# One FFN matmul fewer between a digit's counts and their sum in the second routing round

## The chip, the cores and the metric

The kernel runs on one core of a Trainium2 chip. The metric is the device time of one execution in microseconds (us); the median of several executions is quoted. Engines: TensorE (PE, its weight loads PEld), VectorE (DVE), ScalarE (ACT), GpSimd (POOL), SyncE (SP). A list of executions also gives each one's span (the time, less some 1.8 us) and its mean granted TensorE clock, where 1 is full speed.

## The reference, cut to what matters

```python
y = gated_linear_attention(q, k, v, f_logit)       # 4 batches, 8 heads, 768 steps, 48 wide
x = y.transpose(0, 2, 1, 3).reshape(3072, 384)     # one row per token
logits = x @ w_gate                                # 3072 x 8 experts
for idx in np.argsort(-logits.flatten()):          # greedy, best pair first
    tok, e = idx // 8, idx % 8
    if assigned[tok] < 0 and counts[e] < 384:      # each expert takes 384 tokens
        assigned[tok] = e; counts[e] += 1
for e in range(8):
    h = np.maximum(x[assigned == e] @ w1[e], 0)    # 384 -> 1024
    out[assigned == e] = h @ w2[e]                 # 1024 -> 384
```

## The kernel before: the parts that matter

After the attention part the routing runs in eight rounds, numbered 0 to 7. A round searches a threshold digit by digit (five digits), makes the list of one expert's tokens, gathers their rows and puts that expert's FFN, in 51 pieces, into a queue. A piece is a transposition of 128 gathered rows (three transposes), or one FFN matmul in fp32 (two records in the trace). TensorE takes pieces from the queue at fixed places of the next round, beside the small matmuls of the search.

```python
def digit_beside(above, choice, size, slots):
    some(pe_work, slots[0])              # FFN pieces before the counts
    ...                                  # three matmuls "cnt" (L758): the counts
    ...                                  # VectorE: own, part, parts
    some(pe_work, slots[1])              # FFN pieces between counts and their sum
    nc.tensor.matmul(out=cnt, lhsT=ones[0:m, :], rhs=parts...)      # the sum (L773)
    ...                                  # VectorE: fills, filled, sized, the next digit's "above"

def assign(choice, over, pick, slots):
    ...
    some(pe_work, slots[0])
    nc.tensor.matmul(out=r[:, 0:E], lhsT=ones[:], rhs=count[:], ...)   # "sums" (L819)
    some(pe_work, slots[1])

def tokens():                            # the list is made; its rows are gathered
    ...
    pieces, last = ffn(L), []
    if len(pe_work) >= 12:               # hold two old matmuls back, between the transposes
        last = [pe_work.pop() for _ in range(2)][::-1]
    pe_work.extend(pieces[:TE - 1] + last[:1] + pieces[TE - 1:TE] + last[1:] + pieces[TE:])

pace = {0: None, 1: (2, 2)}
for rnd in range(E - 1):
    slots, more = pace.get(rnd, (3, 2)), 3 if rnd > 1 else 0
    ...                                  # five digits, the first with `more` pieces more
    assign(choice, over, pick, (3, 7))
    ...                                  # nine steps of the list, with 1 or 2 pieces after each
```

## Time and profile before

| | before |
|---|---|
| time, three runs | 478.16 us (477.72 to 478.54) |
| span of the profiled run | 474.0 us, mean clock 0.967 |
| TensorE busy | 93% of the span |
| VectorE, ScalarE, GpSimd busy | 55%, 29%, 28% |
| list to list, rounds 2 to 6 | 36.9 to 37.0 us, once 38.62 |

The rows of waits name who waited for whom, and the order of work gives each instruction's start and length, with the idle time before it in brackets. Two consecutive records of an FFN matmul start 0.32 us apart though each is shown 0.5 us long, because a record runs to a modelled end; so the idle times are somewhat short. The lines themselves stand in the prediction.

### The profile page before, as it was taken

To read this page: it belongs to the slowest core of one execution; us is meant where nothing else is said; L and a number is where in the kernel's file an instruction comes from. 1 tells how busy PE (TensorE), PEld (TensorE's weight loads), DVE (VectorE), ACT (ScalarE), POOL (GpSimd) and SP (SyncE) were. 2 spreads that over 40 slices of the span, in tenths; PEclk is the share of its full clock that TensorE was granted. 3 is DMA by queue.
4 is the path that set the end of the run, shared out by engine and by line. 5 is a ranking of instruction groups with operands and counts; after the bars stand their busy time and mean duration, and the time that the engine had idled before them with its cause. 6 is when DMAs were issued, how large, how long until landed. Compare 5 with 4: busy or idle time off the path is not lost. (4 is left out here: it accounts for less than half of the span.)

```text
span 474.0 us, 11870 instructions
## 1 busy us (share of the span) xinstructions
PE 439.3 (93%) x4854; PEld 296.1 (62%) x4854; DVE 262.2 (55%) x890; ACT 139.0 (29%) x322; POOL 131.3 (28%) x190
## 2 busy tenths in 40 slices
PE   8999999999998489998998998998998998999994
PEld 4788889899887344554564564554554555555552
DVE  5788767788796757555555636726735656000000
ACT  4666646566641011102202202212202211212200
POOL 1556546565530030051042023023014015201001
PEclk9999989999999569999999999999998999999998
DMA  8999988888111071271071082072072046800001
GB/s 171 204 202 201 198 188 179 176 176 191 55 46 54 3 253 64 67 256 44 13 293 62 0 297 70 0 283 83 2 271 94 1 168 193 324 0 35 17 17 39
DMA packets 118399, 59.11 MB, mean 125 GB/s; under 512 B 101664, under 2 KB 112960, under 8 KB 118336
## 3 DMA queue, kind: packets, MB, share of 16 engines
q1 hardware_dynamic: 111760, 44.06, 35.4%
q0 software_dynamic: 3072, 9.44, 6.1%
q10 hardware_dynamic: 3504, 4.77, 2.8%
q8 instruction: 40, 0.66, 0.6%
q14 instruction: 23, 0.19, 0.1%
HBM read 48.77 MB, written 9.49 MB: 123 GB/s over the span
## 5 line engine op out<-in xcount | busy, mean ns | idle before, releaser
L1021 PE MATMUL H<-xeT,w 128*128 128x384 f32 x384 | 136.7, 503 | 4.0 <-ACT xeT L1013 4.0
L1021 PEld LDWEIGHTS H<-xeT,w 128*128 128x128 f32 x384 | 68.6, 192 | 45.8 <-issue 6.2
L1038 POOL DMA_INDIRECT out_dram<-o,token x21 | 22.6, 1074 | 204.8 <-ACT o L1037 200.6
L1033 PE MATMUL O<-w,hT 128*128 128x384 f32 x192 | 64.8, 489 | 0.0
L1033 PE MATMUL last_O<-w,hT 128*128 128x384 f32 x192 | 64.7, 489 | 0.0
L1025 ACT ACTIVATE hT<-H 128x384 f32<-128x384 f32 x64 | 31.4, 490 | 113.0 <-PE H L1021 113.0
L1033 PEld LDWEIGHTS last_O<-w,hT 128*128 128x128 f32 x192 | 35.9, 190 | 25.0 <-issue 1.4
L1033 PEld LDWEIGHTS O<-w,hT 128*128 128x128 f32 x192 | 35.8, 190 | 24.0 <-issue 0.7
L313 DVE COPY_PREDICATED am<-mask,A 128x512 f32<-128x512 int32 x48 | 32.4, 731 | 14.6 <-PE A L308 14.6
L237 POOL TENSOR_TENSOR kg<-k,ek 128x384 f32<-128x384 f32 x23 | 23.1, 1004 | 49.3 <-ACT ek L215 49.3
L308 PE MATMUL A<-qT,kT 48*64 48x128 f32 x768 | 26.8, 273 | 1.1 <-ACT gl L247 0.7
L323 PE MATMUL Y<-v,am 128*64 128x48 f32 x768 | 27.0, 223 | 0.3 <-DVE am L313 0.3
L323 PEld LDWEIGHTS Y<-v,am 128*64 128x64 f32 x768 | 24.6, 138 | 1.4 <-DVE am L313 0.8
L978 POOL DMA_INDIRECT xe<-xd,token x21 | 22.3, 1060 | 8.4 <-issue 4.3
L191 POOL TENSOR_TENSOR low<-g,upper 128x384 fp32r<-128x384 f32 x22 | 22.2, 1008 | 7.3 <-DVE upper L188 5.6
L308 PEld LDWEIGHTS A<-qT,kT 48*64 48x64 f32 x768 | 21.4, 133 | 1.8 <-issue 0.9
L1013 ACT COPY xeT<-Xe 128x384 f32<-128x384 f32 x24 | 11.3, 480 | 36.9 <-PE Xe L1010 36.8
L127 PE MATMUL nothing<-idle,ones 128*128 128x384 bf16 x77 | 20.4, 408 | 1.7 <-DVE ones L132 1.5
L1037 ACT COPY o<-O 128x384 f32<-128x384 f32 x12 | 5.7, 478 | 54.2 <-PE O L1033 54.2
L1037 ACT COPY o<-last_O 128x384 f32<-128x384 f32 x11 | 5.3, 478 | 54.6 <-PE last_O L1033 48.6
L214 ACT ACTIVATE eq<-dl 128x384 f32<-128x384 f32 x24 | 12.6, 524 | 27.4 <-DVE dl L212 27.4
L1010 PE MATMUL Xe<-ident,xe 128*128 128x128 f32 x72 | 12.4, 286 | 6.8 <-DMA xe<-xd,token 6.8
(218 smaller groups left out, 648.2 us busy)
## 6 DMA issues: line engine op xcount, KB each, us to landing
w<-in_moe_w_dram SPq DMA_DIRECT2D x16, 1536.0 KB, 6.7
f<-in_f_logit_dram SPq DMA_DIRECT2D x24, 192.0 KB, 4.3
q<-in_q_dram SPq DMA_DIRECT2D x24, 192.0 KB, 3.8
k<-in_k_dram SPq DMA_DIRECT2D x24, 192.0 KB, 4.4
v<-in_v_dram SPq DMA_DIRECT2D x24, 192.0 KB, 3.6
xd<-x ACTq DMA_DIRECT2D x24, 192.0 KB, 2.9
xe<-xd,token POOLq DMA_INDIRECT x21
out_dram<-o,token POOLq DMA_INDIRECT x21
```

The costliest lines, as they stand in the source:

```text
L127: nc.tensor.matmul(out=nothing[:, 0:CAP], lhsT=ones[:], rhs=idle[:], start=True, stop=True)
L191: nc.gpsimd.tensor_tensor(out=low[:], in0=g[:, :, 0:DH], in1=upper[:].bitcast(FP32), op=ALU.subtract)
L214: nc.scalar.activation(out=G["eq"][:], in_=dl[:], func=AF.Exp, bias=0.0, scale=-1.0)
L237: engine.tensor_tensor(out=G["kg"][:, :, 0:DH], in0=G["k"][:], in1=G["ek"][:], op=ALU.mult)
L308: nc.tensor.matmul(out=A[par][HC * j:HC * j + HC, 128 * hp:128 * hp + 128], lhsT=G["kT"][rows, hp, HC * j:HC * j + HC], rhs=G["qT"][rows, ...
L313: nc.vector.copy_predicated(am[:, par], mask[:].unsqueeze(1).to_broadcast((128, HP, 128)), A[par][:].rearrange("s (a t) -> s a t", t=128))
L323: nc.tensor.matmul(out=Y[par][HC * j:HC * j + HC, DH * hp:DH * hp + DH], lhsT=G["am"][:, par, hp, HC * j:HC * j + HC], rhs=G["v"][:, 2 * h ...
L978: nc.gpsimd.indirect_dma_start(out=xe[:], out_offset=None, in_=xd[:, :], in_offset=bass.IndirectOffsetOnAxis(ap=token[:, i:i + 1], axis=0))
L1021: nc.tensor.matmul(out=L["H"][:, 0:CAP], lhsT=L["w1"][:, d, 128 * ft:128 * ft + 128], rhs=xT[:, d, :], start=(d == 0), stop=(d == DC - 1))
L1025: nc.scalar.activation(out=hT[:, ft, :], in_=L["H"][:, 0:CAP], func=AF.Relu)
L1033: nc.tensor.matmul(out=L["O"][:, 0:D], lhsT=hT[:, ft, 128 * i:128 * i + 128], rhs=L["w2"][:, ft, :], start=(ft == 0), stop=(ft == FC - 1))
L1038: nc.gpsimd.indirect_dma_start(out=outs[next(tiles)][:, :], out_offset=bass.IndirectOffsetOnAxis(ap=L["token"][:, i:i + 1], axis=0), in_=o ...
```

## The change

Round 1 has fewer FFN pieces to spare than later rounds, since nothing was left from round 0. The intent is to use one less in each of its digits, so that more are left when its list is made and TensorE has work until the rows arrive.

```diff
-            pace = {0: None, 1: (2, 2)}
+            pace = {0: None, 1: (2, 1)}
```

## The prediction

> **What bounds the kernel now.** I read the page first, then TensorE's waits from 176 us on, TensorE's order of work in the second and third round, and the granted clock around one stall. The page says who is busy:
>
> ```profile
> PE 439.3 (93%) x4854; PEld 296.1 (62%) x4854; DVE 262.2 (55%) x890; ACT 139.0 (29%) x322; POOL 131.3 (28%) x190
> ```
>
> TensorE sets the end, so only its idle time can be won. The kernel has an attention part (up to some 154 us), which the change does not touch, and a routing part of eight rounds, numbered here 0 to 7. A round finds one expert's tokens on VectorE and GpSimd while TensorE works off the FFN of the expert before, taken piece by piece from a queue. What TensorE waits for in the routing part (columns: who waited for whom, us in total, times, longest):
>
> ```profile
> PE Xe L1010 <- DMA xe<-xd,token: 6.8, 11, 0.9
> PE H L1021 <- ACT xeT L1013: 4.0, 7, 0.6
> PE cnt L758 <- DVE above L527: 1.1, 4, 0.3
> PE sums L819 <- DVE count L530: 1.1, 6, 0.2
> PE before L892 <- DVE member L524: 0.3, 1, 0.3
> ```
>
> The first two are one bubble: TensorE reaches the transposes of the gathered rows (L1010) before the gather has landed, and the first FFN matmul (L1021) then waits for ScalarE's copy of the transposes. In time order, at the start of round 2 (start us, us, engine, line, what; in brackets the idle time before):
>
> ```profile
> 207.48 0.75 PE L963 MATMUL tokens<-number,in_line 128*128 128x6 bf16 x24
> 208.08 5.41 PE L1033 MATMUL O<-w,hT 128*128 128x384 f32 x16
> 213.33 0.25 PE L758 MATMUL cnt<-choice,above 128*128 128x64 bf16 x3
> 213.41 0.53 PE L1010 MATMUL Xe<-ident,xe 128*128 128x128 f32 x3
> 214.37 0.55 PE L1010 MATMUL Xe<-ident,xe 128*128 128x128 f32 x3 [0.43 <-DMA xe<-xd,token]
> 214.76 0.22 PE L773 MATMUL cnt<-parts,ones 128*128 128x128 bf16 x1
> 215.74 0.55 PE L1010 MATMUL Xe<-ident,xe 128*128 128x128 f32 x3 [0.76 <-DMA xe<-xd,token]
> 216.85 1.56 PE L1021 MATMUL H<-xeT,w 128*128 128x384 f32 x4 [0.57 <-ACT xeT L1013]
> 218.25 0.25 PE L758 MATMUL cnt<-choice,above 128*128 128x64 bf16 x3
> ...
> 221.75 0.25 PE L758 MATMUL cnt<-choice,above 128*128 128x64 bf16 x3
> ```
>
> The list of tokens is made at 207.48. Only 8 FFN matmuls (16 records, two to a matmul) lie between it and the transposes. The gather's issues on GpSimd:
>
> ```profile
> 211.22 0.97 POOL L978 DMA_INDIRECT xe<-xd,token  x1 [0.30 <-issue]
> 212.49 1.10 POOL L978 DMA_INDIRECT xe<-xd,token  x1 [0.30 <-issue]
> ```
>
> The second ends at 212.19 and its transposes start at 214.37; the third 213.59, then 215.74. So rows are there 2.2 us after the issue ends. Rounds 2 to 7 show the same three gaps (0.3 to 0.5, 0.6 to 0.9 and 0.57 us).
>
> Now round 1, where the change is; one digit:
>
> ```profile
> 185.12 0.26 PE L758 MATMUL cnt<-choice,above 128*128 128x64 bf16 x3 [0.29 <-DVE above L527]
> ...
> 185.98 0.29 DVE L520 TENSOR_TENSOR parts<-part,pick_th 128x128 bf16<-128x128 bf16 x1
> ...
> 186.59 0.22 PE L773 MATMUL cnt<-parts,ones 128*128 128x128 bf16 x1
> ...
> 188.44 0.26 PE L758 MATMUL cnt<-choice,above 128*128 128x64 bf16 x3 [0.29 <-DVE above L527]
> ```
>
> From counts to sum (185.12 to 186.59) TensorE is the later one: the parts are done at 186.27, but two FFN matmuls stand ahead of the sum. From sum to the next counts (1.86 us) VectorE is.
>
> **What the Trainium skill says.** "DMA: Bandwidth & Descriptors", section on the anatomy of a GpSimd DMA, gives a fixed cost of about 2 us; "Perfetto Trace Analysis", summary of the profiler window, says such a record ends when the descriptors are generated, not when data has moved. Both agree with the 2.15 to 2.2 us above. "TensorE: Matmul & The Clock Gate", "What's actually happening", says that TensorE's clock falls to half after an idle window, and that windows of 3413 ns run freely. The trace has this once in the routing part, right after round 6's bubble, for some 3.4 us (window; time, busy PE, PEld, DVE, ACT, POOL; then the clock):
>
> ```profile
> 364.50:365.00 0.50, 0.21 (x1) 0.22 (x2) 0.09 (x1) 0.23 (x1) 0.00 (x0) 0.63 0.00 0
> 367.50:368.00 0.50, 0.50 (x5) 0.49 (x4) 0.09 (x1) 0.00 (x0) 0.00 (x0) 0.50 0.00 0
> ```
>
> Lists are at 207.48, 244.47, 281.44, 318.37, 355.36 and 393.98: rounds of 36.9 to 37.0 us, and one of 38.62. The dip costs 1.65 us.
>
> **The change part by part.** It takes one FFN matmul from each of round 1's five digits. Replaying the queue by hand: round 0 adds 51 pieces (3 transposes, 24 up, 24 down) and uses 2. Round 1 takes 5x4 for digits, 10 around its sums and 11 up to the list: 8 are left. With (2, 1) it is 5x3, and 13 are left. Rounds 2 to 6 each take as many as they add, 51, so every later list finds 13 too instead of 8. And the code that holds the last two matmuls back, to put them between the transposes, needs at least 12; it never applied up to round 6 and now applies everywhere.
>
> Sizes: an FFN matmul is 0.645 us (8 of them, 451.66 to 456.82, take 5.16); plus 0.09 after counts (218.33 to 219.71 is two, 1.38) and 0.055 after a sum (219.76 to 221.75 is three, 1.99); a transpose piece is 0.33 (two, 433.72 to 434.37).
>
> *Round 1.* The sum starts when the parts are done (counts + 1.15 + 0.06 for the signal = 1.21) instead of at 1.47: 0.26 saved in four digits. In the first, parts end at 179.56, so 179.62 for 179.94: 0.32. The list is 1.36 us earlier. VectorE's 1.86 us stays.
>
> *Rounds 2 to 6*, from the list at 0. Before: counts 5.85, next counts 10.77, third counts 14.27 (221.75 - 207.48). After: tokens and 8 down matmuls again, counts at 5.85; two down matmuls, sum at 7.31; one down matmul and two transposes end at 7.37 + 0.70 + 0.65 = 8.72, but VectorE lets the counts start only at 7.31 + 1.86 = 9.17 (a new wait, 0.45); one down matmul and the third transposes end at 10.31, sum at 10.38; the last down matmul and two up end at 10.44 + 0.70 + 1.29 = 12.43, the third counts. The copy of the transposes is ready at 9.98 + 1.11 = 11.09 (from 215.74 to 216.85), before the up matmuls at 11.14. The same work is done at the third counts in both, so each round saves 14.27 - 12.43 = 1.84; five save 9.20.
>
> The gather is not late: the store that stood before it on GpSimd (208.43) now comes after, so issues start about 1.4 after the list, and rows land at about 4.7, 6.0 and 7.3 for use at 8.07, 8.4 and 9.98.
>
> *Round 7.* VectorE still sets the matmul "before" at 5.68 (399.66 - 393.98); 4 down matmuls and 2 transposes end at 9.03, the second list waits for VectorE's last in_line (403.00, so 9.08), then down, transposes, down, and up matmuls from 11.54, where the copy is ready. Before, they went on at 11.27 (405.25) with two of them done. So the end lies 11.54 + 1.29 - 11.27 = 1.56 later after round 6's list; that is the five deferred matmuls (3.2) less the bubble.
>
> Sum: -1.36 - 9.20 + 1.56 = -9.0 us. In TensorE's idle time: about 2 us more in round 1, 11 us less later.
>
> *Clock.* Without the bubble I expect no dip. The bubbles come 37 us, or 10.8 windows, apart, so they walk through the window's phases in six rounds and about one should be hit in most runs. I count 0.8 x 1.65 = 1.3 us, and take off 0.4 for what I have not seen: 478.16 - 9.0 - 1.3 + 0.4 = 468.3.
>
> **Rivals.** (1) Only time moved: five matmuls are deferred, TensorE is 93% busy, and round 1 loses as much as is won, about 478. Against it: 10.8 us of waits stand in the first two rows of the waits, and all but round 1's go. (2) The new wait is larger: with fewer matmuls beside it, VectorE's digit chain becomes the bound, in round 1 and in the second digit of each later round. That is in my sum (0.39 and 0.45 us a time); were it double in the later rounds, 2.6 us would go, leaving some 471. (3) The gather lands later since it now runs beside other transfers; it has over 2 us of slack, so it would take twice the issue-to-landing time to cost anything. (4) The clock: dips in more rounds of the timed runs than of the profiled one (475.83 against 478.16 us) would make the gain larger, 466 or 467; low activity in round 1 could bring a new dip, but TensorE still works about 72% of each digit there.
>
> **Range and chances.** The sum without the clock is 469.2, with one dip removed 467.5; 2% is 468.6, just between. The sum's own errors are some 0.2 us in each of five rounds. Range 466.2 to 471.0. Over 2% faster 0.54, within 2% 0.45, slower 0.01.
>
> **What would show it.** In the changed profile: the wait of L1010 for the gather gone from the waits, that of L1021 for the copy near zero except round 1's; a new wait of the sum (L773) for parts, about 0.2 to 0.4 us, in round 1; counts to counts there 3.06 instead of 3.32 us; lists from round 1 to 6 35.1 us apart; third counts 12.4 us after each list; a wait of under 0.5 us before each round's second counts; no clock of 0.5 after 180 us. Wrong it would be if the lists stay 37 us apart (the gather is late all the same) or TensorE's waits for VectorE grow past 5 us in total.

## The result, and the profile after

| | before | after |
|---|---|---|
| time, four runs each | 477.94 us (477.39 to 478.54) | 465.36 us (464.15 to 466.11) |
| span of the profiled run | 474.0 us | 462.9 us |

The ratio is 0.9734 (95% interval 0.9707 to 0.9761): the mean time of one kernel's fast runs over that of the other's of the same rounds, so not quite the ratio of the medians. The kernel is 2.7% faster. The direction was right; the time lies 0.8 us below the stated range.

The page of the kernel after, its line for the engines' busy time:

```profile
PE 435.3 (94%) x4854; PEld 293.7 (63%) x4854; DVE 263.5 (57%) x890; ACT 138.6 (30%) x322; POOL 131.6 (28%) x190
```

The work is the same and the span shorter. TensorE's waits after 176 us, as who waited for whom, total us, times, longest:

```profile
PE cnt L758 <- DVE above L527: 2.6, 9, 0.3
PE sums L819 <- DVE count L530: 1.1, 6, 0.2
PE cnt L773 <- DVE parts L520: 1.0, 5, 0.2
PE H L1021 <- ACT xeT L1013: 0.6, 1, 0.6
PE Xe L1010 <- DMA xe<-xd,token: 0.2, 1, 0.2
```

The wait of the transposes for the gather falls from 6.8 to 0.2 us and that of the first up matmul for the copy from 4.0 to 0.6; what is left of both is round 1's own. Two small waits for VectorE take their place. The start of round 2 in order of time:

```profile
205.82 0.75 PE L963 MATMUL tokens<-number,in_line 128*128 128x6 bf16 x24
...
211.67 0.25 PE L758 MATMUL cnt<-choice,above 128*128 128x64 bf16 x3
...
213.18 0.86 PE L1033 MATMUL O<-w,hT 128*128 128x384 f32 x2
213.88 0.82 PE L1010 MATMUL Xe<-ident,xe 128*128 128x128 f32 x6
214.98 0.26 PE L758 MATMUL cnt<-choice,above 128*128 128x64 bf16 x3 [0.28 <-DVE above L527]
215.08 0.89 PE L1033 MATMUL O<-w,hT 128*128 128x384 f32 x2
215.81 0.49 PE L1010 MATMUL Xe<-ident,xe 128*128 128x128 f32 x3
...
218.26 0.25 PE L758 MATMUL cnt<-choice,above 128*128 128x64 bf16 x3
```

Counts at 211.67 - 205.82 = 5.85 after the list, second counts at 9.16, third at 12.44; the prediction had 5.85, 9.17 and 12.43. The transposes are reached with all rows there, and a down matmul (L1033) stands between the second and the third. A digit of round 1:

```profile
184.27 0.26 PE L758 MATMUL cnt<-choice,above 128*128 128x64 bf16 x3 [0.29 <-DVE above L527]
...
185.13 0.29 DVE L520 TENSOR_TENSOR parts<-part,pick_th 128x128 bf16<-128x128 bf16 x1
...
185.47 0.22 PE L773 MATMUL cnt<-parts,ones 128*128 128x128 bf16 x1 [0.21 <-DVE parts L520]
```

The sum now waits for the parts and starts 1.20 us after the counts, instead of 1.47.

### The profile page after: what moved, and what is told of

Read it like the earlier page. It is cut to its first block, busy times and chain, and to the rows that moved or that the text cites. A ratio compares the mean times of both kernels' runs of the same rounds, so it can differ in the third digit from the quotient of the medians.

```text
span 462.9 us, 11870 instructions
## 1 busy us (share of the span) xinstructions
PE 435.3 (94%) x4854; PEld 293.7 (63%) x4854; DVE 263.5 (57%) x890; ACT 138.6 (30%) x322; POOL 131.6 (28%) x190
## 5 line engine op out<-in xcount | busy, mean ns | idle before, releaser
L1021 PE MATMUL H<-xeT,w 128*128 128x384 f32 x384 | 133.7, 496 | 0.6 <-ACT xeT L1013 0.6
L1033 PE MATMUL O<-w,hT 128*128 128x384 f32 x192 | 67.5, 493 | 0.0
L1033 PE MATMUL last_O<-w,hT 128*128 128x384 f32 x192 | 67.1, 492 | 0.0
L1033 PEld LDWEIGHTS last_O<-w,hT 128*128 128x128 f32 x192 | 35.1, 190 | 22.7 <-issue 1.7
L1033 PEld LDWEIGHTS O<-w,hT 128*128 128x128 f32 x192 | 34.9, 190 | 21.7 <-issue 1.4
L1038 POOL DMA_INDIRECT out_dram<-o,token x21 | 21.3, 1012 | 78.9 <-ACT o L1037 76.7
L936 POOL TENSOR_TENSOR block<-past 128x72 f32<-128x72 f32 x8 | 2.4, 300 | 120.7 <-DVE at L527 108.4
L978 POOL DMA_INDIRECT xe<-xd,token x21 | 20.4, 971 | 14.8 <-DVE used L524 8.3
L214 ACT ACTIVATE eq<-dl 128x384 f32<-128x384 f32 x24 | 12.6, 524 | 26.6 <-DVE dl L212 26.6
L263 ACT COPY qT<-T 128x512 f32<-128x512 f32 x24 | 14.1, 586 | 12.6 <-PE T L255 10.0
```

Source lines behind the costliest of these rows:

```text
L263: nc.scalar.copy(out=G["qT"][:].rearrange("p a t -> p (a t)"), in_=G["qTs"][:])
L978: nc.gpsimd.indirect_dma_start(out=xe[:], out_offset=None, in_=xd[:, :], in_offset=bass.IndirectOffsetOnAxis(ap=token[:, i:i + 1], axis=0))
L1021: nc.tensor.matmul(out=L["H"][:, 0:CAP], lhsT=L["w1"][:, d, 128 * ft:128 * ft + 128], rhs=xT[:, d, :], start=(d == 0), stop=(d == DC - 1))
L1033: nc.tensor.matmul(out=L["O"][:, 0:D], lhsT=hT[:, ft, 128 * i:128 * i + 128], rhs=L["w2"][:, ft, :], start=(ft == 0), stop=(ft == FC - 1))
L1038: nc.gpsimd.indirect_dma_start(out=outs[next(tiles)][:, :], out_offset=bass.IndirectOffsetOnAxis(ap=L["token"][:, i:i + 1], axis=0), in_=o ...
```

## The experiments

Theory A: the missing gain is clock. The bubble of the kernel before also lets TensorE's clock fall to half more often than the one trace at hand had shown. Theory B: it lies elsewhere, in the attention part or the end. Besides, the two parts of the mechanism, the number left over and the holding back, were to be told apart. All runs gave correct results. The kernels of a first batch ran on one chip (17 runs of before there, six of them as e1), those of a second on another (11 runs of before). "Lost clock" below is (1 - mean clock) x span, as the mean over runs. Most of it is common to both kernels: every trace shows half clock for 17 or 20 us from some 152 to 159 us on (rounds 0 and 1), and again after TensorE's last matmul. A "dip" is one of the short stretches of some 3.4 us besides. At a margin of 2%, e1, e2 and e4 come out as the same as before, e7 and e8 as faster, and e3, e5 and e6 as unclear, since their intervals reach across 0.98; what those three show is read from their traces.

**e1_before_again.** No edit.

> The kernel before, unchanged, to see its plain executions one by one. The prediction's sum for the pair of profiled runs was 9.0 us of TensorE idle time and 1.65 us for one dip of the clock; the two traces differ by 11.1. The timed runs differ by 12.6, so some 1.5 us is missing. Theory A (clock): the profiled run of before (span 474.0, clock 0.967) was a lucky one; its usual run has two or more dips in rounds 2 to 7, so spans near 476 at a mean clock near 0.963, and a new trace shows two or more stretches at clock 0.5 after 200 us. Theory B (elsewhere): usual runs have the same clock as the profiled one, at most one dip after 200 us, and the extra 2 us lie in the attention part or in the end.

Measured: 477.7 us median of 6 runs, 475.68 to 482.17; the 11 other runs of before beside it 474.75 to 480.52. So three runs within 0.8 us had hidden a scatter of several us. The clock goes with it: the run of 475.68 has 0.976, that of 482.17 has 0.961. The trace has two dips, in rounds 2 and 5, with list-to-list distances of 38.62 and 38.67 us. The first of them, by windows of 2 us (width, busy PE, PEld, DVE, ACT, POOL, clock, DMA):

```profile
216.00:218.00 2.00, 2.00 (x4) 1.09 (x5) 0.00 (x0) 0.00 (x0) 0.00 (x0) 0.50 0.03 8
218.00:220.00 2.00, 2.00 (x9) 1.06 (x8) 0.79 (x3) 0.14 (x1) 0.00 (x0) 0.70 0.00 0
```

At most four records in the first 2 us, where a full clock has six. This speaks for theory A, as far as one trace can.

**e2_before_warm.** `idle_turns(n, X)` are n matmuls of nothing, written into a bank that the next real matmul overwrites; only experts 1 to 6 have them.

```diff
                     X = bank("Xe", "H")
+                    idle_turns((0, 2, 4)[i] if 0 < L["place"] < 7 else 0, X)
...
                         L["H"] = bank("H", "H")
+                        if ft == 0 and 0 < L["place"] < 7:
+                            idle_turns(3, L["H"])
```

> The kernel before, with 9 matmuls of nothing (bf16, 0.16 us each) put into the bubble of rounds 2 to 7 (2 before the second transposes, 4 before the third, 3 before the first up matmul), where TensorE only waits. The bubble stays as long, but TensorE is busy in it. Theory A: no dips of the clock after 180 us, lists 37.0 us apart in every round, and the time falls by the dips alone: two of 1.65 us make 474.7 for 477.9 (one dip: 476.3, three: 473). Theory B: the time stays within 0.5 us of 477.9.

Measured: 474.99 us median of 6 runs, ratio to before 0.9945 (0.9901 to 0.999). Lists stay 37.0 to 37.1 us apart, and no stretch of half clock is in rounds 2 to 7 of its trace. The bubble in round 2, filled:

```profile
216.11 0.81 PE L127 MATMUL Xe<-idle,ones 128*128 128x384 bf16 x4
217.12 0.55 PE L1011 MATMUL Xe<-ident,xe 128*128 128x128 f32 x3 [0.20 <-DMA xe<-xd,token]
217.51 0.65 PE L127 MATMUL H<-idle,ones 128*128 128x384 bf16 x3
```

TensorE has more work, and rows and copies come no earlier, yet the mean time is 2.7 us lower (interval some 0.5 to 4.7), and the mean lost clock is 12.4 us against some 15. That is near theory A's figure for two dips (474.7); the interval is wide enough for one or almost three.

**e3_after_nohold.** The kernel after, with the hold-back off up to round 6.

```diff
-                if len(pe_work) >= 12:
+                if len(pe_work) >= 40:
```

> The kernel after without holding the last two FFN matmuls back between the transposes in rounds 1 to 6 (13 are left, in plain order). By the prediction's way of counting, from the list at 0: sum 7.31, three down matmuls, counts 9.35, two transposes, sum 10.56, third transposes 10.62, up matmuls only at 11.73 because they wait for the copy, third counts 13.05, against 12.43 with the holding back: 0.62 lost in each of five rounds and 0.6 in round 7, so 3.7 us slower than after, 469.0. Rival (holding back does nothing, only the number left matters): 465.4, as after.

Measured: 468.07 us, ratio to before 0.9789. Every list-to-list distance of rounds 2 to 6 is 35.78 us, against 35.15 or 35.16 after: 0.63 for 0.62 counted. From round 6's list to the last group of FFN matmuls it takes 70.06 us, against 69.30. The traces so show 5 x 0.63 + 0.76 = 3.9 us; the mean times differ by only 2.7 (468.0 against 465.4 in ten runs of after), on different chips, and this kernel's runs lost 1.1 us less clock. The start of its round 2 has the wait in which the 0.62 lies:

```profile
217.04 0.50 PE L1010 MATMUL Xe<-ident,xe 128*128 128x128 f32 x3
218.11 1.56 PE L1021 MATMUL H<-xeT,w 128*128 128x384 f32 x4 [0.57 <-ACT xeT L1013]
```

Without a matmul between transposes and up matmuls, TensorE waits for ScalarE's copy again.

**e4_before_hold.** The kernel before with the hold-back on.

```diff
-                if len(pe_work) >= 12:
+                if len(pe_work) >= 8:
```

> The kernel before with holding back alone: its limit lowered from 12 to 8, so that of the 8 left two go between the transposes. Counted: six down matmuls end at 4.6, the first transposes wait for rows until 5.6, the second until 6.9 and now stand before the first counts (7.2 instead of 5.85), the third at 8.3, second counts 10.72 against 10.77: nothing won, within 0.5 us of 477.9. Rival (the interleaving is what helps, not the number left): lists under 36.2 us apart and a time below 474.

Measured: 476.2 us, ratio to before 0.9959 (0.991 to 1.0007). The median is 1.3 us below that of before, outside the 0.5 that I allowed, but its mean lost clock is also lower (12.9 us), and the distances of its lists are 36.92 to 36.99 us, with one of 38.34 where the clock dips: nothing won. The waits have only moved to the first and second transposes:

```profile
215.82 0.55 PE L1010 MATMUL Xe<-ident,xe 128*128 128x128 f32 x3 [0.88 <-DMA xe<-xd,token]
217.06 0.55 PE L1010 MATMUL Xe<-ident,xe 128*128 128x128 f32 x3 [0.70 <-DMA xe<-xd,token]
```

So holding back is worth nothing when too few are left, and 0.63 us a round when enough are.

**e5_after_again.** No edit to the kernel after.

> The kernel after, unchanged, beside the kernel before on one chip, to split the gain by the clocks of the single runs. Theory A (clock): besides the 9.0 us of bubble, before's runs lose more clock than after's; (1 - mean clock) x span was 15.0 us as the mean of 17 runs of before and 12.3 of after's four, so a difference of 2 to 3.5 us here and a ratio near 0.974. If the clock counted as the prediction said (0.8 dips), the difference is 1.4 us and the ratio 0.978.

Measured: 465.38 us median of 6 runs; before beside it 477.48; ratio 0.9765 (0.9725 to 0.9805), between the two figures. The lost clock is 12.06 us here and 14.47 for before: a difference of 2.4, within theory A's 2 to 3.5; with a standard error of 0.6 it does not alone exclude the 1.4 of the prediction's count. The trace again has 35.15 or 35.16 us in each of rounds 2 to 6, and no half clock in them.

**e6_one_two.** The piece taken from the other place of the digit.

```diff
-            pace = {0: None, 1: (2, 2)}
+            pace = {0: None, 1: (1, 2)}
```

> Round 1 with (1, 2) instead of (2, 1): again one FFN matmul fewer for a digit and 13 left, but taken from before the counts, where VectorE's chain is the later one, and not from before the sum. By the prediction's working the digits then stay at 3.32 us, list to list stays at 39.7 us in round 1 (38.4 after), and everything later is as after: rounds 35.15 us, so 1.3 us slower than after. Rival (only the number left counts, the place doesn't): list to list 38.4 us in round 1 and the time of after.

Measured: 466.58 us, ratio to before 0.9807; the mean is 1.6 us above that of after in the same batch, which is about as large as the scatter of the runs. The trace is sharper: 39.70 us from round 0's list to round 1's, as before, and later rounds as after. The counts wait 0.9 us for VectorE in a digit, so each deferred matmul leaves a hole of its own size. The place from which it is taken is worth 1.3 us.

**e7_after_sums.** The kernel before with five pieces fewer in round 1 behind the sums.

```diff
-                (assign_exact if exact else assign)(choice, over, pick, (3, 7))
+                (assign_exact if exact else assign)(choice, over, pick, (3, 2 if rnd == 1 else 7))
```

> The kernel before with its (2, 2), and 2 instead of 7 FFN matmuls after the sums of round 1, where VectorE waits for the matmul behind them: 13 are left too, without idle time of TensorE in the digits. Round 1's list should come 5 x 0.645 = 3.2 us earlier than before (36.5 us after round 0's, for 39.7 before and 38.4 after), later rounds as after at 35.15 us: 1.9 us faster than after. Rival (VectorE needs that time for the list): list to list above 37.5 us, no gain over after.

Measured: 463.43 us, the mean 2.0 us below that of after in the same batch. Round 1's list comes 36.53 us after round 0's, and the later rounds take 35.15 or 35.16. The matmuls can be deferred where nothing else is on the critical path behind them; VectorE had waited 3.85 us there for the matmul at their end.

**e8_best.** A version to beat both.

```diff
-            pace = {0: None, 1: (2, 2)}
+            pace = {0: None, 1: (3, 1)}
...
-                first, counted = 0, None
+                first, counted = first // 3, None
...
-                (assign_exact if exact else assign)(choice, over, pick, (3, 7))
+                (assign_exact if exact else assign)(choice, over, pick, (4, 1 if rnd == 1 else 5))
...
-            some(pe_work, 4)
+            some(pe_work, 5)
```

> A version meant to beat both: 13 left by way of round 1's last part as in the run before, (3, 1) in round 1, in rounds 2 to 6 one matmul more before the second counts (where after waits 0.45 us for VectorE) and one more before the sums (0.37 us), two fewer after them, and one more at the start of round 7. Counted: round 1's list 35.7 us after round 0's, rounds of 34.3 us, 0.3 less in round 7: some 7 us faster than after, 458. If TensorE's waits only move elsewhere: rounds stay above 35 us and the time above 463.

Measured: 459.07 us, ratio to before 0.9622 (0.9582 to 0.9661), the mean 6.6 us below that of after. Lists 35.72 us from round 0 to 1, and 34.38 or 34.39 in rounds 2 to 6. Of TensorE's waits after 170 us only round 1's are left:

```profile
PE cnt L773 <- DVE parts L520: 1.0, 5, 0.2
PE H L1021 <- ACT xeT L1013: 0.6, 1, 0.6
```

**e9_look1 to e9_look4.** Four more traces of the kernel before, no edit.

> The kernel before once more, one execution for its trace: how many of the six bubbles of rounds 2 to 7 are followed by a stretch at half clock. The clocks of 28 runs of before and 10 of after differ by 2.6 us of lost clock, 1.5 dips of 1.7 us. If those dips are the bubbles', the four looks together have some 6 (4 to 8), each in a list-to-list distance of 38.3 to 38.7 us in place of 37.0; at the 0.8 that the prediction counted, 3; if they lie in the attention part or at the end, 0 to 2.

> As the first look: the second of four, together some 6 dips in rounds 2 to 7 by theory A, 3 at the prediction's count, 0 to 2 if the dips lie elsewhere.

> As the first look: the third of four, together some 6 dips in rounds 2 to 7 by theory A, 3 at the prediction's count, 0 to 2 if the dips lie elsewhere.

> As the first look: the last of four, together some 6 dips in rounds 2 to 7 by theory A, 3 at the prediction's count, 0 to 2 if the dips lie elsewhere.

Measured: 475.16, 475.29, 478.23 and 479.39 us, with 1, 0, 2 and 1 dips in rounds 2 to 6, at list-to-list distances of 38.55 to 38.66 us. That is four together: the low end of theory A's 4 to 8, and nearer to 3 than to 6. With the first trace (1) and e1 (2), six traces of before have 7 dips in these rounds, 1.17 each, all behind a bubble. The seven traces at hand whose bubble is gone, much shorter or filled (after, e2, e3, e5, e6, e7, e8) have none there. The run e4, whose bubble only moved, has one. (The four are single runs, whose state is unknown; only their count of dips is used. A fifth run of before beside them, without a trace, took 473.29 us.) In the attention part the six have 4 dips and the seven also 4.

## Why the prediction was right or wrong

**The bubble: right.** The working gave -1.36, -9.20 and +1.56. Measured from list to list, so without what the attention part does by chance: round 1 took 38.42 and 38.30 us in two traces of after, for 39.70, which is -1.28 and -1.40. Rounds 2 to 6 took 35.15 or 35.16, for 36.99 without a dip, so 1.84 each and 9.2 in all. From round 6's list to the last group it took 69.30, for 68.0, +1.3. The sum is -9.2 for the -9.0 predicted. Only the last term was off, by 0.3: I let the final up matmuls start 11.54 us after round 6's list, and they start at 392.86 - 381.60 = 11.26. One reading was loose: round 7 of before has two of the three gaps (0.86 and 0.57 us), not three.

**The order of the queue: right.** That 8 became 13 in every round, and that the limit of 12 is passed by it, follows from the queue; e4 and e3 show that both are needed. The number alone leaves 0.63 us a round, the holding back alone everything.

**The new waits: right in place, and not a rival.** The sum in round 1 waits 0.15 to 0.22 us for the parts, and the second counts of rounds 2 to 6 wait 0.28 us for "above" (0.45 by starts). The rows were in time, as counted: GpSimd's issues started at 207.24, 1.42 us after the list.

**The clock: the mechanism right, the size wrong.** This is the step that failed: "one should be hit in most runs. I count 0.8 x 1.65 = 1.3 us, and take off 0.4", so 0.9 us for the clock. The size of a dip was right (38.55 to 38.67 us for 37.0). Their number was not: six traces have 1.17 in a mean, and none is left after. That is 1.17 x 1.65 = 1.9 us. By the clocks of all runs, 28 of before and 10 of after, the lost clock is 14.8 and 12.2 us, a difference of 2.6 with a standard error of 0.6. The 0.4 taken off for the unseen had nothing behind it. In the mean over these runs the time falls from 477.5 to 465.4, 12.1 us with a standard error of 0.5; 9.2 of bubble and 2.6 of clock make 11.8, where the prediction had 9.0 and 0.9. Side by side on one chip (e5) the means fall by 11.4 us with an error of 0.7, so the 12.6 of the first comparison, from four runs each, lies above both. I had the hint in hand: the profiled run of before was 2.3 us faster than the median, which my fourth rival turned into "466 or 467", but I gave it little weight. A mean of 1.17 dips is not far from 0.8, so part of the miss is the run-to-run scatter, which three close runs had hidden and the range ignored. The prediction also says that the trace has half clock "once in the routing part"; the same trace has it from 153.0 to 173.5 us too, but so has the kernel after.

The kept traces also show which bubble is hit. In each, all changes of the clock after the first 2 us and before TensorE's last matmul lie on one grid of 3.413 us: in that of before, half clock starts at 64.26, 153.00 and 364.62 us, 26 and 62 steps apart. Cut by its own grid, each of the six traces of before shows TensorE busy for 48 to 53% of the step before each of the 7 dips in rounds 2 to 6, and for 57% or more of every other full-clock step from 180 to 430 us (0.516 before the dip at 364.62; 0.612 at the least elsewhere in that trace). A dip came where one step held all three gaps of a bubble, that is, where a step ended 9.20 to 9.45 us after the list; where it ended at 9.00 or earlier, or at 10.28 or later, none came. In the seven traces without the bubble no step of that stretch falls below 70%. So the prediction's picture of bubbles that walk through the window holds; it counted the hits too low (e1 and e9_look3 were hit twice, in rounds 2 and 5). e4 shows that the limit is not sharp: of two steps of 53%, one was followed by a dip.

**The rivals.** That only time is moved is out by the 12 us; a doubled new wait and a late gather by the figures above. The fourth, more dips in usual runs, is what happened in part.

**What stays open.** The traces place 1.9 us of the clock's share in the rounds; the other 0.7 of the 2.6 is within its error, and no trace shows it as the change's work: the long half-clock stretch after 153 us costs 9.7 us of lost clock in the mean of the six traces and 9.5 in that of the seven. That the dips come from the bubble is shown by e2 and by their places on the grid; no run has shifted the grid against the bubble on purpose.

**What the skill was used for.** What "Perfetto Trace Analysis" says of the end of a GpSimd gather's record fits here. The fixed cost of about 2 us in "DMA: Bandwidth & Descriptors" fits less well than the prediction says: the page counts the setup in it, while the 2.2 us are counted from the record's end; from its start it is 3.1 us (211.22 to 214.37). That rows need 2.2 us after the issue's end is what made the eight matmuls too few. The half clock and the 3.4 us window of "TensorE: Matmul & The Clock Gate" fit each dip seen.

## What to carry to other kernels

When the bounding engine works off a queue beside a chain on another engine, look at how much is left in the queue at the moment a new wait starts: a few pieces deferred once are inherited by every later round. Take them from a place where the other engine isn't the later one (here behind the sums rather than in a digit), and keep one or two for the gaps between dependent steps. Several short bubbles close together can cost the clock beside their own length (here three within 3.4 us), so look at the clock of several runs before giving a range.

## What the Trainium skill lacked or had wrong

- "TensorE: Matmul & The Clock Gate", "What's actually happening", has the clock fall after at least one idle window of about 3.4 us. Here it fell after windows in which TensorE is never shown idle for more than about 0.9 us at a time and still did its transposes (three gaps of some 0.4, 0.8 and 0.57 us), in 7 of the 30 bubbles in rounds 2 to 6 of six traces. The page does name frequent micro-idling in another section, but gives no share of busy time at which it starts: here windows shown busy for 48 to 53% were followed by half clock, and those of 57% or more were not. Filling the gaps with nine matmuls of nothing left no dip in the one trace of it.
- "Perfetto Trace Analysis" says that a TensorE record's end is estimated; it does not say that waits then look shorter. Here a wait shown as 0.28 us was 0.45 us by the starts, from 213.88 plus 0.65 for two transpositions to 214.98.
